# Attention and mixture of experts on one core: expert ranks by turns, two product groups in a bank, the overflow list by partitions

## The chip, the cores and the metric

The program runs on one core of a Trainium2 chip. The metric is the device time of a run in microseconds (us). Engines: PE is TensorE, with PEld its weight loads; DVE is VectorE, ACT ScalarE, POOL GpSimd, SP SyncE, whose queue issues most of the transfers.

## What is computed

Clustered attention on 4 batches, 8 heads, 768 positions of 64: queries and keys get the nearest of 16 centroids, and a query sees the keys of its own. The 3072 tokens of 512 numbers then go through 4 groups of 4 experts, one expert a token:

```python
for g in range(G):
    xg = x[g_idx == g]
    ...
    for e in range(Eg):
        ...
        h = np.maximum(xg[mask_e] @ w1[g, e], 0.0)
        ye = h @ w2[g, e]
        ...
        out[tok_idx] = combined[:, None] * ye
```

`w1[g, e]` is 512 x 1024, `w2[g, e]` 1024 x 512.

## The kernel before

Attention takes the first 400 us and isn't touched, apart from constants that POOL makes in it (`setup`, L985, near 98 us). Matrices are kept as two float16 parts, high and low, and a product of two is three matmuls.

The largest expert is begun early ("part A", 288 tokens, and a rest of 128 that is called rank -1). The other 15 are sorted by their count of tokens (`order`, L1327). Rank k has a fixed capacity `caps[k]` (L976): 288 for the largest, 272, 256 and so on down to 160 and 160. Tokens over the capacity go to an overflow list (`lists`, L1366, `make_list`, L1413), which `rest` works off at the end if it isn't empty; here it is.

`ranks` (L1464) runs rank -1 to 14. In a step, `up` (L1223) of rank k and `down` (L1242) of rank k-1 take turns, 12 matmuls each. `up` makes 8 groups of 12 matmuls, M = `caps[k]` columns each, into PSUM banks `psh` (three, a group a bank). ACT evicts a group as `hh`, DVE the rest as `hl` (L1238, L1239). `down` makes four groups of 24 into `psy` (two banks), evicted by ACT as `yh` and by DVE as `yl` (L1261, L1262); `settle` (L1284) turns them back to rows with products on `back`, ACT scales them to `y` (L1300) and POOL scatters the rows (L1301). For capacities of 240, 256 and 128 `feature_major` (L1278) picks the other form, 512-column products and no settle.

Around this, in fixed places of a step: POOL gathers the tokens of the next rank (L1193); PE transposes them and ACT copies them to `xT` (L1208, L1209); `stream` (L1159) loads the weights in chunks of 512 KB, six ahead, and splits them: the high part on ACT or POOL (L1019, L1021), the low part on DVE (L1022). The weights of two ranks fit at a time. `late` hands out one piece of the list a step, from rank 2 on (L1491 to L1493), on DVE, with one partition. The bank pool `psm` has three banks, for transposes, settles and the small products.

The order of instructions on each engine is set by a scheduler, from the order of the program and what it reckons each takes. An engine works off its instructions in that order.

Of the kernel before, what the change touches and what calls it, by code (L numbers as in the profile page):

```python
# [11 lines left out]
F16 = mybir.dt.float16  # L12
# [10 lines left out]
P = 128  # L23
# [929 lines left out]
class Experts:  # L953
# [13 lines left out]
    def __init__(self, ctx, tc, R, w1, w2, out, stage, wa):  # L967
        self.tc, self.R, self.w1, self.w2, self.out = tc, R, w1, w2, out
        self.nc = tc.nc
        self.D = out.shape[1]  # L970
        self.F = math.prod(w1.shape[1:]) // self.D
        self.stage, self.wa, self.stage2, self.nst = stage, wa, None, 0
        E = R.E
        const = self.const = ctx.enter_context(tc.tile_pool(name="econst", bufs=1))
        nc = self.nc
        self.caps = [288, 272, 256, 240, 232, 224, 216, 208, 200, 192, 184, 176, 168, 160, 160, self.CA]  # L976
        assert max(self.caps) == SL and len(self.caps) == E and not any(c % 8 for c in self.caps)
        self.sizes = [[min(P, c - t * P) for t in range(-(-c // P))] for c in self.caps]
        sm = self.small = lambda name, shape, dt=F32: const.tile(shape, dt, name=name)
        self.oh0 = sm("oh0", [P, E])  # L980
        self.cntA = sm("cntA", [P, E])
        self.f0f = sm("f0f", [P, 1])
        self.f0i = sm("f0i", [P, 1], I32)

    def setup(self):  # L985
        nc, const, E = self.nc, self.const, self.R.E
        self.io = const.tile([P, E], F32, name="io")
        nc.gpsimd.iota(self.io, [[1, E]], base=0, channel_multiplier=0, allow_small_or_imprecise_dtypes=True)
        self.capr = const.tile([1, E], F32, name="capr")
# [233 lines left out]
    def up(self, xT, M, W, h):  # L1223
# [5 lines left out]
        h += [hh, hl]  # L1229
        for f in range(FC):  # L1230
            fs = slice(f * P, (f + 1) * P)
            ph = next(self.ps_h).tile([P, 512], F32, name="psh")
            i = 0
            for k in range(KD):
                for w, a in ((w1h, 0), (w1h, 1), (w1l, 0)):
                    self.mm = nc.tensor.matmul(out=ph[:, 0:M], lhsT=w[:, k, fs], rhs=xT[:, a, k], start=i == 0, stop=i == 3 * KD - 1)  # L1236
                    i += 1
            nc.scalar.activation(out=hh[:, f], in_=ph[:, 0:M], func=AF.Relu)  # L1238
            self.ev = nc.vector.scalar_tensor_tensor(out=hl[:, f], in0=ph[:, 0:M], scalar=0.0, in1=hh[:, f], op0=ALU.max, op1=ALU.subtract)  # L1239
            yield  # L1240

    def down(self, h, M, W, gcols, idcols):  # L1242
# [4 lines left out]
        if self.feature_major(M):  # L1247
# [79 lines left out]
    def order(self):  # L1327
# [9 lines left out]
        c = sm("ocol", [V, 2])  # L1337
        nc.vector.tensor_tensor(out=t, in0=key, in1=R.emask, op=ALU.mult)
# [4 lines left out]
        nc.vector.scalar_tensor_tensor(out=self.pick, in0=self.io[0:V].unsqueeze(1).broadcast_to([V, 2, E]), scalar=c[:, 1:2], in1=R.wv.broadcast_to([V, 2, E]), op0=ALU.is_equal, op1=ALU.mult)  # L1343
# [22 lines left out]
    def lists(self):  # L1366
# [15 lines left out]
        yield
        done = self.done = sm("done", [1, E + 1])
        nc.vector.tensor_tensor(out=pe, in0=t.broadcast_to([1, E, E]), in1=self.io[0:1].unsqueeze(1).broadcast_to([1, E, E]), op=ALU.is_equal)
        nc.vector.tensor_tensor(out=pe, in0=pe, in1=self.capr.unsqueeze(1).broadcast_to([1, E, E]), op=ALU.mult)
        nc.vector.tensor_reduce(out=done[:, 0:E], in_=pe, axis=AX.X, op=ALU.add)
        nc.vector.memset(done[:, E:E + 1], float(self.CB))
        self.eid = sm("eid", [1, E + 1])
        nc.vector.tensor_copy(out=self.eid[:, 0:E], in_=self.io[0:1])
        nc.vector.tensor_copy(out=self.eid[:, E:E + 1], in_=self.f0f[0:1])  # L1390
        EB, MJ = E + 1, R.N // P + 1
        MO = self.MO = R.N // P + EB
        self.base = sm("base", [1, EB])
        self.jt = sm("jt", [1, EB, MJ])
        self.jj = sm("jj", [1, MO, EB], F16)
        with self.tc.issue_after(self.got.ins):
            self.iotas(EB, MJ, MO)
        for nm, sh in (("rem", [1, EB]), ("nov", [1, EB]), ("hiE", [1, EB]), ("loE", [1, EB]), ("zer", [1, EB]),
                       ("tmp", [1, MO, EB]), ("lst", [1, 2, MO]), ("sb", [1, EB])):
            setattr(self, "L" + nm, sm("L" + nm, sh))  # L1400
        self.Lgj = self.Ltmp.rearrange("o m e -> o (m e)")[:, 0:EB * MJ].rearrange("o (e m) -> o e m", m=MJ)
        self.Lind = sm("Lind", [1, MO, EB], F16)
        self.Llsi = sm("Llsi", [1, 2, MO], I32)
        self.Lnoi = sm("Lnoi", [1, 1], I32)
        nc.vector.memset(self.Lzer, 0.0)
        yield
        yield from self.make_list()

    def iotas(self, EB, MJ, MO):
        for t, pat in ((self.jt, [[0, EB], [P, MJ]]), (self.base, [[self.R.BS, EB]]), (self.jj, [[1, MO], [0, EB]])):  # L1410
            self.nc.gpsimd.iota(t, pat, base=0, channel_multiplier=0, allow_small_or_imprecise_dtypes=True)

    def make_list(self):  # L1413
        nc, R = self.nc, self.R
        EB, MJ, MO = R.E + 1, R.N // P + 1, self.MO
        V = nc.vector
        V.tensor_tensor(out=self.Lrem, in0=self.c17[0:1], in1=self.done, op=ALU.subtract)
        V.tensor_tensor(out=self.Lgj, in0=self.Lrem.broadcast_to([1, EB, MJ]), in1=self.jt, op=ALU.is_gt)
        V.tensor_reduce(out=self.Lnov, in_=self.Lgj, axis=AX.X, op=ALU.add)
        V.tensor_tensor_scan(out=self.LhiE, data0=self.Lnov, data1=self.Lzer, initial=0.0, op0=ALU.add, op1=ALU.add)  # L1420
        V.tensor_tensor(out=self.LloE, in0=self.LhiE, in1=self.Lnov, op=ALU.subtract)
        yield
        b3 = lambda x: x.unsqueeze(1).broadcast_to([1, MO, EB])
        V.tensor_tensor(out=self.Lind, in0=self.jj, in1=b3(self.LloE), op=ALU.is_ge)
        V.tensor_tensor(out=self.Ltmp, in0=self.jj, in1=b3(self.LhiE), op=ALU.is_lt)
        V.tensor_tensor(out=self.Lind, in0=self.Lind, in1=self.Ltmp, op=ALU.mult)
        yield
        V.tensor_tensor(out=self.Ltmp, in0=self.Lind, in1=b3(self.eid), op=ALU.mult)
        V.tensor_reduce(out=self.Llst[:, 0], in_=self.Ltmp, axis=AX.X, op=ALU.add)
# [4 lines left out]
        V.scalar_tensor_tensor(out=self.Ltmp, in0=self.jj, scalar=float(P), in1=b3(self.Lsb), op0=ALU.mult, op1=ALU.add)  # L1434
        V.scalar_tensor_tensor(out=self.Ltmp, in0=self.Ltmp, scalar=1.0 / 8, in1=self.Lind, op0=ALU.mult, op1=ALU.mult)
        V.tensor_reduce(out=self.Llst[:, 1], in_=self.Ltmp, axis=AX.X, op=ALU.add)
        V.tensor_copy(out=self.Llsi, in_=self.Llst)
        V.tensor_copy(out=self.Lnoi, in_=self.LhiE[:, EB - 1:EB])
# [93 lines left out]
class Fixup:  # L1532
# [24 lines left out]
    def finish(self):  # L1557
# [4 lines left out]
        nc.vector.tensor_tensor(out=any_, in0=self.zf[0:1], in1=X.LhiE[:, X.R.E:X.R.E + 1], op=ALU.add)  # L1562
# [136 lines left out]
```

## Time and profile before

| | |
|---|---|
| median of 3 runs | 739.57 us (739.32 to 740.96) |
| the profiled execution | 742.52 us |
| its span | 740.7 us |
| PE, PEld busy | 97%, 84% |
| DVE, ACT, POOL busy | 80%, 66%, 67% |
| mean granted clock of PE | 0.997 |

The span runs from the first instruction to the last; the time of the execution has some 2 us around it. Busy times of PE are modelled, as its matmuls overlap: what a matmul costs is read from the distance of starts.

### The profile page before, as it was taken

Reading aid. Unit: us, or ns where it says so; the run is one execution under the profiler, and the core shown is the slowest. Engines: PE = TensorE matmul, PEld = TensorE weight load, DVE = VectorE, ACT = ScalarE, POOL = GpSimd, SP = SyncE. Lnnn points to the kernel's source line nnn. Section 1 sums busy time; section 2 is a strip of 40 time slices with the busy share of each in tenths; the row PEclk is TensorE's granted clock in tenths of the full one; section 3 lists DMA queues with packets and bytes.
Section 4 is the critical chain, followed back from the end, with each engine's and each line's share of the span. In section 5 each row is a group of like instructions: output and inputs, shape, how many; then the busy total and the mean of one; then the engine's idle time right before and its main releaser. Section 6 shows DMA issues by size and latency. Waiting matters only on the chain.

```text
span 740.7 us, 26722 instructions
## 1 busy us (share of the span) xinstructions
PE 720.3 (97%) x11106; PEld 619.1 (84%) x11106; DVE 596.1 (80%) x1216; ACT 486.0 (66%) x952; POOL 493.6 (67%) x491
## 2 busy tenths in 40 slices
PE   8899999999999999999999989999999999999996
PEld 4688788888888888888888677888789999999996
DVE  6899889899888997989876476767779889988961
ACT  7778877788778887677977275444454555555642
POOL 8899787777787877878786325354644688554542
PEclk9999999999999999999999999999999999999998
DMA  8955634435245351240521696866777678887921
GB/s 226 224 141 153 192 100 119 155 99 154 81 120 172 95 159 37 67 131 3 178 81 38 234 313 220 273 211 221 237 244 234 230 272 284 284 275 264 281 77 36
DMA packets 45881, 128.04 MB, mean 173 GB/s; under 512 B 7699, under 2 KB 12691, under 8 KB 45752
## 3 DMA queue, kind: packets, MB, share of 16 engines
q1 hardware_dynamic: 40668, 112.64, 49.8%
q0 software_dynamic: 4928, 13.59, 5.1%
q8 instruction: 89, 1.46, 0.8%
q14 instruction: 40, 0.33, 0.1%
q10 hardware_dynamic: 156, 0.03, 0.0%
HBM read 93.41 MB, written 13.65 MB: 145 GB/s over the span
## 4 chain that ended last, share of the span: by engine, by line
PE 67%; DVE 17%; ACT 6%; issue 5%; DMA 2%; POOL 1%; another core or an unknown queue 1%; POOLq 0%; ACTq 0%; DVEq 0%
PE psh L1236 16%; PE psy L1258 12%; DVE mpart L382 7%; PE pso L447 6%; PE psf L421 6%; PE pso L448 5%; PE psf L422 5%; PE psc L379 5%; PE psy L1272 3%; DVE parts L224 2%; ACT p L426 2%; DMA st<-w 2%; PE psm L765 2%; PE psm L1294 1%; PE psm L1208 1%
## 5 line engine op out<-in xcount | busy, mean ns | idle before, releaser
L428 POOL TENSOR_TENSOR pl<-p 128x512 f16<-128x512 f32 x278 | 285.4, 1042 | 75.1 <-ACT p L426 70.6
L382 DVE TENSOR_REDUCE mpart<-psc 128x1 f32<-128x512 f32 (+1 forms) x282 | 190.2, 682 | 28.8 <-PE psc L379 28.4
L426 ACT ACTIVATE p<-psf 128x512 f32<-128x512 f32 x288 | 169.7, 596 | 45.6 <-PE psf L422 40.4
L447 PE MATMUL pso<-V,p 128*128 128x65 f16 x1152 | 160.2, 193 | 0.0
L448 PE MATMUL pso<-V,pl 128*128 128x64 f16 x1152 | 159.9, 193 | 0.0
L447 PE MATMUL pso<-V,pl 128*128 128x65 f16 x1152 | 159.4, 193 | 0.5 <-POOL pl L428 0.5
L448 PE MATMUL pso<-V,p 128*128 128x64 f16 x1152 | 159.3, 193 | 0.0
L421 PE MATMUL psf<-A 82*128 82x384 f16 (+2 forms) x576 | 142.5, 273 | 1.7 <-ACT p L426 1.6
L422 PE MATMUL psf<-B 128*128 128x384 f16 (+2 forms) x576 | 142.7, 273 | 0.0
L448 PEld LDWEIGHTS <-p 128*128 128x128 bf16 x1152 | 112.2, 97 | 22.2
L447 PEld LDWEIGHTS <-p 128*128 128x128 bf16 x1152 | 113.1, 98 | 9.6 <-issue 1.6
L447 PEld LDWEIGHTS <-pl 128*128 128x128 f16 x1152 | 112.5, 98 | 0.6 <-POOL pl L428 0.6
L448 PEld LDWEIGHTS <-pl 128*128 128x128 f16 x1152 | 111.5, 97 | 0.3
L379 PE MATMUL psc<-A 80*128 80x512 f16 (+1 forms) x376 | 106.3, 325 | 1.9 <-DVE mpart L382 1.2
L1239 DVE SCALAR_TENSOR_TENSOR hl<-psh,hh 128x160 f16<-128x160 f32 (+14 forms) x136 | 49.8, 368 | 48.9 <-ACT hh L1238 43.5
L1238 ACT ACTIVATE hh<-psh 128x160 f16<-128x160 f32 (+14 forms) x136 | 45.8, 345 | 59.1 <-PE psh L1236 54.9
L1301 POOL DMA_INDIRECT out_dram<-y,ri x33 | 43.4, 1316 | 52.4 <-ACT y L1300 46.3
L1236 PE MATMUL psh<-xT,wh0a 128*128 128x288 f16 (+7 forms) x512 | 74.6, 255 | 0.0
L1193 POOL DMA_INDIRECT xg<-xbuf,ri x25 | 40.5, 1620 | 43.7 <-PE psm L1208 30.1
L422 PEld LDWEIGHTS <-B 128*128 128x128 f16 x576 | 56.5, 98 | 10.9 <-issue 2.3
L1236 PE MATMUL psh<-xT,wh0b 128*128 128x272 f16 (+6 forms) x448 | 64.7, 253 | 0.0
L1236 PE MATMUL psh<-xT,wl0a 128*128 128x288 f16 (+7 forms) x256 | 64.0, 255 | 0.0
(385 smaller groups left out, 1785.9 us busy)
## 6 DMA issues: line engine op xcount, KB each, us to landing
st<-w SPq DMA_DIRECT2D x128, 512.0 KB
B<-parts SPq DMA_DIRECT2D x60, 192.0 KB
kx<-kT SPq DMA_DIRECT2D x16, 384.0 KB
qx<-qT SPq DMA_DIRECT2D x16, 384.0 KB
vx<-vr SPq DMA_DIRECT2D x16, 384.0 KB
xbuf<-xs SPq DMA_DIRECT2D x4, 1536.0 KB
A<-parts SPq DMA_DIRECT2D x30, 192.0 KB
A<-mk SPq DMA_DIRECT2D x56, 24.0 KB
```

What stands on the lines that cost most here:

```text
L379: last["mm"] = nc.tensor.matmul(out=pc[:, off:off + k1 - k0], lhsT=QA[h % 8][0:80, c * P:(c + 1) * P], rhs=KA[h % 8][0:80, k0:k1], start=T ...
L382: nc.vector.tensor_reduce(out=(mp[:, 0, 0:1], mp[:, :, 1], mp[:, 1, 0:1])[i], in_=pc.rearrange("p (a x) -> p a x", a=n), axis=AX.X, op=ALU ...
L421: nc.tensor.matmul(out=o, lhsT=KA[h % 8][0:82, ks], rhs=QA[h % 8][0:82, q0:q1], start=True, stop=False)
L422: nc.tensor.matmul(out=o, lhsT=KBs[h][:, ks], rhs=QBs[h][:, q0:q1], start=False, stop=True)
L426: cfg["exp"] = nc.scalar.activation(out=p32, in_=pf, func=AF.Exp, scale=QK / (SQ * SQ))
L428: lo = (nc.vector if u in (EARLY if h < 2 else DVE_LO[h % 8] if h < NH - 2 else DVE_END) else nc.gpsimd).tensor_tensor(out=pl, in0=p32, in ...
L447: nc.tensor.matmul(out=O[:, col:col + 65], lhsT=p[:, bs], rhs=vh, start=c == 0 and q == 0 and i == 0, stop=False, skip_group_check=True)
L448: nc.tensor.matmul(out=O[:, col:col + 64], lhsT=p[:, bs], rhs=vl, start=False, stop=c == NCH - 1 and i == 1, skip_group_check=True)
L1236: self.mm = nc.tensor.matmul(out=ph[:, 0:M], lhsT=w[:, k, fs], rhs=xT[:, a, k], start=i == 0, stop=i == 3 * KD - 1)
L1238: nc.scalar.activation(out=hh[:, f], in_=ph[:, 0:M], func=AF.Relu)
L1239: self.ev = nc.vector.scalar_tensor_tensor(out=hl[:, f], in0=ph[:, 0:M], scalar=0.0, in1=hh[:, f], op0=ALU.max, op1=ALU.subtract)
L1258: self.mm = nc.tensor.matmul(out=py[:, 0:M], lhsT=w[:, f, d * P:(d + 1) * P], rhs=a[:, f], start=i == 0, stop=i == len(prods) - 1)
```

## The change

Three edits. (1) `turn` takes the sorted ranks by turns: the largest, the smallest but one, the second, and so on; the capacities from rank 0 are now 288, 160, 272, 168, 256, 176, 240, 184, 232, 192, 224, 200, 216, 208, 160. `at` holds the same table for the chip, which `order` compares with. (2) Where 2M is at most 512, `up` and the feature-major `down` put two groups side by side into one bank, and evict both with one instruction on ACT and one on DVE. (3) The list is made with 128 partitions, an entry on each: operations of 17 columns take the place of ones of up to 697 on one partition, and sums over partitions are small products on PE: `dp`, `np_` and two for `lp`. The three iotas of `lists` go; `setup` makes `at`, `base` and `rows`.

```diff
-        self.caps = [288, 272, 256, 240, 232, 224, 216, 208, 200, 192, 184, 176, 168, 160, 160, self.CA]
+        caps = [288, 272, 256, 240, 232, 224, 216, 208, 200, 192, 184, 176, 168, 160, 160]
+        self.turn = [k // 2 if k % 2 == 0 else E - 3 - k // 2 for k in range(E - 2)] + [E - 2, E - 1]
+        self.caps = [caps[r] for r in self.turn[:-1]] + [self.CA]
...
+        two = 2 if 2 * M <= 512 else 1
         for f in range(FC):
             fs = slice(f * P, (f + 1) * P)
-            ph = next(self.ps_h).tile([P, 512], F32, name="psh")
+            if f % two == 0:
+                pair = next(self.ps_h).tile([P, 512], F32, name="psh")[:, 0:two * M].rearrange("p (t m) -> p t m", m=M)
...
-            nc.scalar.activation(out=hh[:, f], in_=ph[:, 0:M], func=AF.Relu)
-            self.ev = nc.vector.scalar_tensor_tensor(out=hl[:, f], in0=ph[:, 0:M], scalar=0.0, in1=hh[:, f], op0=ALU.max, op1=ALU.subtract)
+            if f % two == two - 1:
+                fs = slice(f + 1 - two, f + 1)
+                nc.scalar.activation(out=hh[:, fs], in_=pair, func=AF.Relu)
+                self.ev = nc.vector.scalar_tensor_tensor(out=hl[:, fs], in0=pair, scalar=0.0, in1=hh[:, fs], op0=ALU.max, op1=ALU.subtract)
...
+                if d % two == two - 1:
+                    ds = slice(d + 1 - two, d + 1)
+                    self.yev.append(nc.scalar.activation(out=yh[:, ds], in_=pair, func=AF.Copy, scale=1.0 / YS))
+                    nc.vector.scalar_tensor_tensor(out=yl[:, ds], in0=pair, scalar=1.0 / YS, in1=yh[:, ds], op0=ALU.mult, op1=ALU.subtract)
...
+        dp = R.psm.tile([P, 512], F32, name="psm")
+        nc.tensor.matmul(out=dp[:, 0:E], lhsT=dw, rhs=R.ident[0:E, 0:E], start=True, stop=True)
...
+        V.tensor_tensor(out=self.Lrem, in0=self.c17, in1=self.done, op=ALU.subtract)
+        V.tensor_scalar(out=self.Lgt, in0=self.Lrem, scalar1=step, scalar2=None, op0=ALU.is_gt)
+        np_ = R.psm.tile([P, 512], F32, name="psm")
+        nc.tensor.matmul(out=np_[:, 0:EB], lhsT=R.ones, rhs=self.Lgt, start=True, stop=True)
+        yield
+        V.tensor_copy(out=self.Lnov, in_=np_[:, 0:EB])
...
+        lp = R.psm.tile([P, 512], F32, name="psm")
+        for w in range(2):
+            nc.tensor.matmul(out=lp[0:1, w * MO:(w + 1) * MO], lhsT=self.Llst[:, w:w + 1], rhs=R.identf[:, 0:MO], start=True, stop=True)
```

Three places show how it moves instructions. First DVE where the list finds what is over (`Lrem`), before:

```order
L1239 SCALAR_TENSOR_TENSOR hl<-psh,hh 128x232
L1022 SCALAR_TENSOR_TENSOR wl1b<-st,wh1b 128x4x256
L1417 TENSOR_TENSOR Lrem<-c_12838,done 1x17
L1418 TENSOR_TENSOR Ltmp<-Lrem,jt 1x425
L1419 TENSOR_REDUCE Lnov<-Ltmp 1x17
L1239 SCALAR_TENSOR_TENSOR hl<-psh,hh 128x232
```

and now, in the rank of 256 (a pair has 512 columns; the lines are those of the changed kernel):

```order
L1255 SCALAR_TENSOR_TENSOR hl<-psh,hh 128x512
L1034 SCALAR_TENSOR_TENSOR wl1b<-st,wh1b 128x4x256
L1432 TENSOR_TENSOR Lrem<-c_12820,done 128x17
L1282 SCALAR_TENSOR_TENSOR yl<-psy,yh 128x336
L1433 TENSOR_SCALAR Lgt<-Lrem,rows 128x17
L1034 SCALAR_TENSOR_TENSOR wl0a<-st,wh0a 128x2x512
```

The reduction that gave `Lnov` on DVE is gone; `Lgt` goes to PE instead. There, where before nothing stood between the products of `up`, it is now, with what each waits for:

```order
L1276 MATMUL psy<-hh,wl1a 128x168
L1250 LDWEIGHTS wh0a
L1250 MATMUL psh<-xT,wh0a 128x256
L1435 LDWEIGHTS ones [waits DVE_49]
L1435 MATMUL psm<-Lgt,ones 128x17 [waits Activation_49]
L1250 LDWEIGHTS wh0a
```

This is one product into the sixth group of `up`; 12 products of `down` (168 columns, L1276), the fifth group and 12 of `down` again stand behind the fourth group, whose pair the `hl` above evicts. Last, ACT at the end of the last rank, before:

```order
L1300 ACTIVATE y<-psm,rg 128x512
L1300 ACTIVATE y<-psm,rg 32x512
L1261 ACTIVATE yh<-psy 128x160 x4
L1300 ACTIVATE y<-psm,rg 128x512
L1300 ACTIVATE y<-psm,rg 32x512
```

and now:

```order
L1320 ACTIVATE y<-psm,rg 128x512
L1320 ACTIVATE y<-psm,rg 80x512
L1281 ACTIVATE yh<-psy 128x320 x2
L1320 ACTIVATE y<-psm,rg 128x512
L1320 ACTIVATE y<-psm,rg 32x512
```

Four evictions of a group have become two of a pair; a product on `back` that reads one half of a pair now stands on PE behind the eviction of both.

## Rows read from the trace of the kernel before

**Rows 1.** The page, busy time, share of the span, instructions

```profile
span 740.7 us, 26722 instructions
...
PE 720.3 (97%) x11106; PEld 619.1 (84%) x11106; DVE 596.1 (80%) x1216; ACT 486.0 (66%) x952; POOL 493.6 (67%) x491
```

**Rows 2.** Windows from one rank's first `up` product to the next's

```profile
core 0: us, PE busy (x) PEld busy (x) DVE busy (x) ACT busy (x) POOL busy (x), PEclk, DMA share, GB/s
...
460.76:484.54 23.78, 23.78 (x211) 19.68 (x208) 16.95 (x22) 10.87 (x20) 11.06 (x12) 1.00 0.81 267
...
609.59:627.96 18.37, 18.37 (x226) 18.37 (x225) 17.70 (x30) 10.20 (x20) 15.10 (x10) 1.00 0.84 274
627.96:645.69 17.73, 17.73 (x227) 17.73 (x226) 16.35 (x27) 9.84 (x20) 10.37 (x8) 1.00 0.89 293
...
695.25:711.20 15.95, 15.84 (x235) 15.70 (x233) 13.49 (x25) 8.58 (x21) 7.91 (x6) 1.00 0.69 217
```

**Rows 3.** Chain of waits in order of time (start, us, what)

```profile
445.66 1.47 PE psh L1236 x12
...
654.51 0.95 PE psh L1236 x12
```

**Rows 4.** Timeline around three pauses (start, length, engine, line, idle before)

```profile
434.79 0.38 PE L1272 MATMUL psy<-wl1a,hh 128*128 128x512 f16 x1
...
435.30 0.68 DVE L1239 SCALAR_TENSOR_TENSOR hl<-psh,hh 128x128 f16<-128x128 f32 x3
...
435.63 0.27 PE L1236 MATMUL psh<-xT,wh 128*128 128x128 f16 x2 [0.46 <-DVE hl L1239]
...
683.50 0.35 DVE L1262 SCALAR_TENSOR_TENSOR yl<-psy,yh 128x184 f16<-128x184 f32 x1 [1.60 <-ACT yh L1261]
683.53 0.24 PE L1236 MATMUL psh<-xT,wl0a 128*128 128x168 f16 x1
683.90 0.77 PE L1258 MATMUL psy<-hh,wh1a 128*128 128x176 f16 x8
...
699.37 0.34 DVE L1262 SCALAR_TENSOR_TENSOR yl<-psy,yh 128x176 f16<-128x176 f32 x1 [0.53 <-ACT yh L1261]
...
699.41 0.23 PE L1236 MATMUL psh<-xT,wl0b 128*128 128x160 f16 x1
699.76 0.45 PE L1258 MATMUL psy<-hh,wh1b 128*128 128x168 f16 x4
```

**Rows 5.** Groups by shape, 440 us on (xcount, busy us, mean ns, idle)

```profile
L1022 DVE SCALAR_TENSOR_TENSOR wl1b<-st,wh1b 128x1024 f16<-128x1024 f32 x30 | 44.7, 1489 | 0.0
L1239 DVE SCALAR_TENSOR_TENSOR hl<-psh,hh 128x160 f16<-128x160 f32 x16 | 5.1, 318 | 7.2 <-ACT hh L1238 7.1
L1239 DVE SCALAR_TENSOR_TENSOR hl<-psh,hh 128x288 f16<-128x288 f32 x8 | 3.6, 454 | 5.0 <-ACT hh L1238 3.0 <-ACT wh1b L1019 1.9
...
L1238 ACT ACTIVATE hh<-psh 128x160 f16<-128x160 f32 x16 | 4.8, 306 | 8.3 <-PE psh L1236 6.9 <-issue 1.4
L1238 ACT ACTIVATE hh<-psh 128x288 f16<-128x288 f32 x8 | 3.2, 403 | 3.4 <-PE psh L1236 3.4
```

**Rows 6.** Timeline at the end of the last rank

```profile
733.08 0.33 DVE L1262 SCALAR_TENSOR_TENSOR yl<-psy,yh 128x160 f16<-128x160 f32 x1 [1.51 <-ACT yh L1261]
...
733.47 0.29 PE L1294 MATMUL psm<-back,yl 128*128 128x128 f16 x2
```

**Rows 7.** Groups of DVE, the list's lines, 460 to 700 us

```profile
L1424 DVE TENSOR_TENSOR Lind<-jj,LloE 1x697 f16<-1x697 f16 x1 | 0.9, 872 | 0.0
...
L1417 DVE TENSOR_TENSOR Lrem<-c,done 1x17 f32<-1x17 f32 x1 | 0.2, 159 | 0.0
```

**Rows 8.** Timeline of POOL near 98 us

```profile
98.60 0.15 POOL L988 IOTA io<- 128x16 f32 x1
```

**Rows 9.** Lines L1553 and L1554 (ns min/median/max, first and last start)

```profile
L1553 PE MATMUL psm<-zh,ones x1: 167/167/167, 636.9 to 636.9; 128*128 128x1 f16 x1
...
L1554 DVE COPY zf<-psm x1: 145/145/145, 640.3 to 640.3; 128x1 f32<-128x1 f32 x1
```

More of the change, by code (lines that the diff above doesn't have):

```diff
@@ L975, in __init__ @@
         nc = self.nc
-        self.caps = [288, 272, 256, 240, 232, 224, 216, 208, 200, 192, 184, 176, 168, 160, 160, self.CA]
-        assert max(self.caps) == SL and len(self.caps) == E and not any(c % 8 for c in self.caps)
+        caps = [288, 272, 256, 240, 232, 224, 216, 208, 200, 192, 184, 176, 168, 160, 160]
+        self.turn = [k // 2 if k % 2 == 0 else E - 3 - k // 2 for k in range(E - 2)] + [E - 2, E - 1]
+        self.caps = [caps[r] for r in self.turn[:-1]] + [self.CA]
+        assert sorted(self.turn) == list(range(E)) and max(self.caps) == SL and len(self.caps) == E and not any(c % 8 for c in self.caps)
         self.sizes = [[min(P, c - t * P) for t in range(-(-c // P))] for c in self.caps]
@@ L1386, in lists @@
[L1386 to L1402, printed above, removed]
+        V = nc.vector
@@ new lines, in lists @@
+        EB, MO = E + 1, R.N // P + E + 1
+        self.MO = MO
+        c = self.c17 = sm("c17", [P, EB])
+        t = sm("lt", [P, E])
+        V.tensor_tensor(out=t, in0=R.cnt, in1=self.oh0, op=ALU.mult)
+        V.tensor_reduce(out=c[:, E:EB], in_=t, axis=AX.X, op=ALU.add)
+        V.tensor_tensor(out=t, in0=self.cntA, in1=R.cnt, op=ALU.subtract)
+        V.tensor_tensor(out=t, in0=t, in1=self.oh0, op=ALU.mult)
+        V.tensor_tensor(out=c[:, 0:E], in0=R.cnt, in1=t, op=ALU.add)
+        dn = sm("dn", [E, E])
@@ L1403, in lists @@
+        V.tensor_copy(out=done[:, 0:E], in_=dp[:, 0:E])
+        V.memset(done[:, E:EB], float(self.CB))
+        self.eid = sm("eid", [P, EB])
+        V.tensor_copy(out=self.eid[:, 0:E], in_=self.io)
+        V.tensor_copy(out=self.eid[:, E:EB], in_=self.f0f)
+        for nm in ("rem", "nov", "hiE", "loE", "zer", "tmp", "sb", "ind"):
+            setattr(self, "L" + nm, sm("L" + nm, [P, EB]))
+        self.Lgt = sm("Lgt", [P, EB], F16)
+        self.Llst = sm("Llst", [P, 2])
         self.Llsi = sm("Llsi", [1, 2, MO], I32)
@@ L1404, in lists @@
         self.Lnoi = sm("Lnoi", [1, 1], I32)
[L1405 removed]
+        V.memset(self.Lzer, 0.0)
         yield
         yield from self.make_list()
[L1409 to L1411 removed]
     def make_list(self):
         nc, R = self.nc, self.R
[L1415 removed]
+        EB, MO = R.E + 1, self.MO
@@ L1416, in make_list @@
         V = nc.vector
-        V.tensor_tensor(out=self.Lrem, in0=self.c17[0:1], in1=self.done, op=ALU.subtract)
-        V.tensor_tensor(out=self.Lgj, in0=self.Lrem.broadcast_to([1, EB, MJ]), in1=self.jt, op=ALU.is_gt)
-        V.tensor_reduce(out=self.Lnov, in_=self.Lgj, axis=AX.X, op=ALU.add)
+        row, step = self.rows[:, 0:1], self.rows[:, 1:2]
+        V.tensor_tensor(out=self.Lrem, in0=self.c17, in1=self.done, op=ALU.subtract)
+        V.tensor_scalar(out=self.Lgt, in0=self.Lrem, scalar1=step, scalar2=None, op0=ALU.is_gt)
@@ L1424, in make_list @@
[L1424 to L1429, printed above, removed]
+        V.tensor_scalar(out=self.Ltmp, in0=self.LloE, scalar1=row, scalar2=None, op0=ALU.is_le)
@@ L1430, in make_list @@
+        V.scalar_tensor_tensor(out=self.Lind, in0=self.LhiE, scalar=row, in1=self.Ltmp, op0=ALU.is_gt, op1=ALU.mult)
+        V.tensor_tensor(out=self.Ltmp, in0=self.Lind, in1=self.eid, op=ALU.mult)
+        V.tensor_reduce(out=self.Llst[:, 0:1], in_=self.Ltmp, axis=AX.X, op=ALU.add)
         yield
```

65 lines of the change are left out of this document (33 added, 32 removed).

## The prediction, made before the changed kernel ran

> **What bounds the kernel now.** I read four views in this order: the page's busy times, the windows (one stretch per rank of the expert part), the chain of waits, and the timeline wherever TensorE (PE) pauses. The span is 740.7 us and PE is busy 97% of it [rows 1]. A busy PE need not be at its pace, so the windows come next, cut where each rank's `up` begins: from 460.76 to 711.20 us PE's busy time equals the stretch to 0.2 us, at a granted clock of 1.00, which is the 2.4 GHz level [rows 2]. The chain confirms it by start times: a group of 12 products of 288 columns takes 1.47 us, 122 ns each, and one of 184 columns 0.95 us, 79 ns each [rows 3]; that is columns / 2.4 GHz plus 2 to 2.5 ns. So a rank costs what its columns cost. VectorE (DVE) is nearly full in some stretches, 17.70 of 18.37 us [rows 2], but PE never slows with it, except at the few pauses below. The expert part is PE's, and only what changes PE's work, its pauses or the end after its last product can show.
>
> **The turns: 0 us.** The caps are the same numbers in another order, the choice of `down`'s form depends on the cap alone, and gathers, transposes and settles go with the cap. A stretch holds `up` of one rank and `down` of the one before. Before, stretches shrink from 23.78 to 15.95 us [rows 2]; by the pitch above, 96 products of 160 columns (6.6 us), 96 of 288 (11.8 us) and some 1.3 us of transposes and settles make about 19.7 us, so now all are near 19. Sum: unchanged. The demand on the weight stream (eight 512 KB chunks a rank) becomes even; the shortest stretch before already held at 15.95 us with PE full, so 19 us should be covered by the transfers and splits. If that cover failed, it would be in the early ranks (rival C).
>
> **The pairs: -1.1 us of pauses.** Two groups now share a bank, so two `psy` banks hold four groups and three `psh` banks six. Three pauses show what that frees: PE stops after 683.53 until 683.90 while DVE's `yl` of 683.50 to 683.85 frees the bank; the same at 699.41 to 699.76; and at 434.79 to 435.63 it waits for `hl`, three small evictions behind a split [rows 4]. Less one pitch each (0.07, 0.07 and 0.22 us) that is 0.30, 0.28 and 0.62 us. I take the first two whole, and 0.5 of the last, since ScalarE (ACT) is full there too: -1.1, at most -1.2, at least -0.6.
> An eviction of 160 columns takes 318 ns on DVE and 306 on ACT, of 288 columns 454 and 403 [rows 5]: 1.06 and 0.76 ns a column, with some 0.15 and 0.18 us for each instruction. Some 78 instructions fewer on either engine (56 of `up`, 22 of `down`) are about 12 us of DVE and 14 of ACT. They are worth 0 beyond the pauses, because PE runs at its pace without them.
> [...]
> At the end pairing costs: the last two groups of the last rank are evicted only together. Before, `yl` of 160 columns began at 733.08, and the settling product that reads it started at 733.47 [rows 6]. Now ACT takes 306 + 160 x 0.76 = 428 ns and DVE 318 + 160 x 1.06 = 488 ns, so 0.29 us more before the last settling products, of which two more than before then remain ahead of the first output copy (0.11 us): **+0.4 us**, between 0.3 and 0.6.
>
> **The list.** Its long one-partition operations, such as 872 ns for 697 elements, give way to ones of 17 columns; one of these took 159 ns [rows 7]. DVE gains over 10 us, worth 0 as above. The iotas that leave GpSimd (POOL) late cover nothing. Seven small instructions and one memset more on POOL near 98 us, at 0.15 us for an iota [rows 8], make at most 1.2 us there, beside an attention pass in which POOL's long operations wait for ACT; I take 0.
> New on PE are four small products (`dp`, `np_`, two of `lp`). The nearest row is the 167 ns of the one-column product on `ones` [rows 9], whose busy time includes its drain; so 0.2 to 0.7 us for four, and I take **+0.4**.
> Three of the four read what DVE made a rank or several evictions earlier. `np_` does not: it reads `Lgt`, which stands on DVE behind `hl` of a 512-column pair, a weight split, `Lrem` and `yl`, in the rank of 256 columns, and the product stands one product into the sixth group of `up` (order shown above). Both sides from the last product of the fourth group: PE has 12 products of 168 columns twice (0.87 us each; in between 12 of 256, 1.31 us) and one more, 3.2 us. DVE has ACT's eviction (about 0.2 us to start, 0.57 long), `hl` 0.69, the split 1.49 [rows 5], `Lrem` 0.16, `yl` of 336 columns 0.50 and `Lgt` 0.16: 3.8 us if nothing queues, and ACT's own split ahead of it may add some. So PE stands still, with every product of the rank behind it: 0.6 us, up to 3 where DVE is as far behind as it was at 640.3 us, when it copied a product started at 636.9 [rows 9]; nothing if the split was done early. I take **+1.0 us**, the nearer end plus part of a queue.
> `np_`'s bank is held for a whole rank; two of three stay for settles and transposes, which here come two at a time: 0.
>
> **Sum.** 0 - 1.1 + 0.4 + 0.4 + 1.0 = +0.7 us. The profiled execution took 742.52 us, so 743.2; the runs' median stands 2.95 us under it, at 739.57: **740.3 us**. All terms at their good ends make -0.7 (738.9); 1.8 us at `np_` and the others at their bad ends +2.5 (742.1). A measurement of this kernel tells a change of over 0.2%, 1.48 us, from none.
>
> **Rivals.**
> A, slower: the wait at `np_` is long. It decides once DVE is about 1 us further behind there than reckoned. For it: DVE lagged 3.4 us at 636.9 to 640.3 [rows 9]. Against it: that was in a fuller stretch, and pairs and turns make this one lighter. At a stall of 3.3 us instead of 1.0: 742.6 us. Chance 0.20.
> B, faster: pauses beyond the three go as well, because a DVE with 12 us less to do releases PE earlier. Against it: PE is full from 460 to 711 us, so only the transition before 443 us has room; with no stall at `np_` and 0.8 us more won there, 740.3 - 1.8 = 738.5, and below 738.1 it counts as faster. Chance 0.10 for faster.
> C, slower: the stream cannot follow, as the second stretch shrinks from 23.78 us to 19.7. Eight chunks are 4.2 MB, 213 GB/s over 19.7 us, against 293 GB/s seen at 627.96 us [rows 2]; if that stretch kept its old length, +4.1, 744.4 us. Chance 0.05.
> That the order does not change as described is excluded by the order of instructions shown above.
>
> **How the numbers follow.** My case, within 0.2%, has 0.65; B 0.10; A 0.20 and C 0.05. The range takes in my case and most of A and B, and leaves out C and their far ends: 738.4 to 742.7.
>
> **What would show it.** The chain should hold the same sum of PE time, with stretches near 19 us; no pause of PE behind `yl` or `hl`; one pause of about 1 us at the product on `Lgt`, near 530 us; DVE's busy time down by some 20 us with no effect; the last `yl` as one of 320 columns, 0.4 us later. It is wrong if PE loses time in many places (pairs evicted too late for the next rank), if the early stretches wait for chunks, or if the time falls by more than the pauses hold.

## The result, and the profile after

The changed kernel took 744.35 us (median of 5 runs, 743.12 to 746.97) against 739.57 us: the ratio is 1.0064, 95% interval 1.0041 to 1.0087, so 3 to 6.4 us slower. Two later measurements gave 1.0068 (1.0046 to 1.0091) and 1.0059 (1.0039 to 1.0079). In all later measurements, on four chips, the kernel before took 742.2 to 742.7 us; so below a ratio is always to the kernel before as it was timed beside the run.

The profiled executions hide most of it. That of before stood 2.95 us over the median of its runs, that of the change 1.2 us under, and the spans differ by 0.7 us only. The page of the changed kernel, beside [rows 1]:

```profile
span 741.4 us, 26582 instructions
...
PE 720.0 (97%) x11112; PEld 619.1 (84%) x11112; DVE 573.5 (77%) x1136; ACT 476.9 (64%) x874; POOL 477.6 (64%) x496
```

PE's busy time is the same to 0.3 us, DVE has 23 us less to do. So the loss is PE standing still, and the pauses are the distance of two starts less the pitch (0.417 ns a column and 2.5 ns, worked out from the two groups of [rows 3]; 2.4 columns a ns, which the prediction writes as 2.4 GHz). The pauses in us, before, in this profile, and in a third profile of the changed kernel (the run `after_c` below):

| place (us of the span) | before | change | `after_c` |
|---|---|---|---|
| part A waits for `yl`, near 424 | 1.86 | 0 | 2.06 |
| rank -1: bank wait, then `xT`, 434 to 440 | 0.63 + 0.46 | 0 + 1.61 | 0 + 1.11 |
| nothing the profile shows, 441 to 446 | 1.28 | 0 | 0.37 |
| `hl` or `hh` late, 455 and 463 | 0 | 0 | 0.32 + 0.92 |
| the product on `Lgt` | - | 1.95 | 1.94 |
| first `down` products wait for `hh`, near 560 and 598 | 0 | 0.79 + 0.21 | 0.96 + 0 |
| `psy` bank, 683 to 731 | 0.76 | 0 | 0 |
| settle of the last rank but one waits for the paired `yl` | 0 | 0.29 | 0.29 |
| last `down` product to the end of the span | 8.2 | 8.8 | 9.1 |

Only the first profile of the change lacks the first row: every other profile of either kernel and of all variants has 1.6 to 2.1 us there. With it, this execution would lie 0.6 us over the median of its runs instead of 1.2 us under.

The windows by rank, beside [rows 2] (columns as there):

```profile
core 0: us, PE busy (x) PEld busy (x) DVE busy (x) ACT busy (x) POOL busy (x), PEclk, DMA share, GB/s
...
457.38:476.87 19.49, 19.49 (x218) 17.12 (x216) 14.61 (x17) 9.63 (x17) 10.57 (x9) 1.00 0.91 304
...
516.70:538.12 21.42, 19.63 (x236) 18.31 (x234) 14.00 (x18) 9.87 (x15) 10.90 (x9) 1.00 0.76 258
...
557.50:576.06 18.56, 17.93 (x210) 17.34 (x208) 13.23 (x18) 9.88 (x15) 9.12 (x8) 1.00 0.76 254
...
651.96:671.05 19.09, 19.09 (x226) 19.09 (x225) 14.28 (x17) 9.66 (x16) 9.15 (x7) 1.00 0.79 271
```

The stretches are even, as the turns mean, and PE is full in most. The rank of 256 (516.70) holds 1.8 us without PE. The waits name it, from 440 to 735 us:

```profile
PEld L1435 <- DVE Lgt L1433: 2.0, 1, 2.0
PE psm L1435 <- DVE Lgt L1433: 1.8, 1, 1.8
...
PE psy L1276 <- ACT hh L1254: 0.6, 1, 0.6
```

What made `Lgt` late stands in the timeline, DVE's and POOL's instructions and the product:

```profile
527.17 0.69 DVE L1255 SCALAR_TENSOR_TENSOR hl<-psh,hh 128x512 f16<-128x512 f32 x1 [1.94 <-ACT hh L1254]
...
527.78 1.22 DVE L1034 SCALAR_TENSOR_TENSOR wl1b<-st,wh1b 128x1024 f16<-128x1024 f32 x1
...
528.52 1.38 POOL L1033 TENSOR_SCALAR wh0a<-st 128x1024 f16<-128x1024 f32 x1
...
528.91 1.01 DVE L1432 TENSOR_TENSOR Lrem<-c,done 128x17 f32<-128x17 f32 x1
...
529.84 0.49 DVE L1282 SCALAR_TENSOR_TENSOR yl<-psy,yh 128x336 f16<-128x336 f32 x1
529.87 1.04 POOL L1033 TENSOR_SCALAR wh1a<-st 128x1024 f16<-128x1024 f32 x1
530.26 0.69 DVE L1433 TENSOR_SCALAR Lgt<-Lrem,rows 128x17 f16<-128x17 f32 x1
...
531.00 0.18 PE L1435 MATMUL psm<-Lgt,ones 128*128 128x17 f16 x1 [1.79 <-DVE Lgt L1433]
```

The queue is the one that the prediction gave, but `Lrem` takes 1.01 us and `Lgt` 0.69 where [rows 7] have 0.16 for such an operation, on one partition and with nothing on POOL beside it. Each ends when a split on POOL ends: 529.92 beside 529.90, 530.95 beside 530.91.

The other new wait is ACT's, ahead of the first `down` of the rank of 176 columns:

```profile
557.57 1.06 ACT L1031 ACTIVATE wh1b<-st 128x1024 f16<-128x1024 f32 x1 [2.36 <-DMA st<-w]
558.53 1.04 ACT L1031 ACTIVATE wh0b<-st 128x1024 f16<-128x1024 f32 x1
559.48 0.44 ACT L1254 ACTIVATE hh<-psh 128x352 f16<-128x352 f32 x1
...
559.97 0.31 PE L1276 MATMUL psy<-hh,wh1a 128*128 128x176 f16 x2 [0.63 <-ACT hh L1254]
```

The last `hh` of the rank stands on ACT behind two splits, and the first of these waits for its chunk. The kernel before has the same order on ACT,

```profile
529.36 1.06 ACT L1019 ACTIVATE wh1b<-st 128x1024 f16<-128x1024 f32 x1 [1.36 <-DMA st<-w]
530.32 1.04 ACT L1019 ACTIVATE wh0b<-st 128x1024 f16<-128x1024 f32 x1
531.27 0.35 ACT L1238 ACTIVATE hh<-psh 128x240 f16<-128x240 f32 x1
```

in the step where `up` of 240 columns runs beside the 512-column `down` of the rank of 256. That step is 22.4 us long (508.32 to 530.68), and PE waits for nothing. Now 176 columns run beside this `down`, in 19.4 us (538.12 to 557.50).

The end, beside [rows 6]:

```profile
732.91 0.44 ACT L1281 ACTIVATE yh<-psy 128x320 f16<-128x320 f32 x1 [2.88 <-PE psy L1276]
733.38 0.49 DVE L1282 SCALAR_TENSOR_TENSOR yl<-psy,yh 128x320 f16<-128x320 f32 x1 [2.83 <-ACT yh L1281]
...
733.93 0.23 PE L1314 MATMUL psm<-back,yl 128*128 128x128 f16 x1 [0.24 <-DVE yl L1282]
```

### The profile page after: what moved, and what is told of

It reads as the page before. It is cut to its first block, busy times and chain, and to the rows that moved or that the text cites. A ratio compares the mean times of both kernels' runs of the same rounds, so it can differ in the third digit from the quotient of the medians.

```text
span 741.4 us, 26582 instructions
## 1 busy us (share of the span) xinstructions
PE 720.0 (97%) x11112; PEld 619.1 (84%) x11112; DVE 573.5 (77%) x1136; ACT 476.9 (64%) x874; POOL 477.6 (64%) x496
## 4 chain that ended last, share of the span: by engine, by line
PE 66%; DVE 17%; ACT 5%; issue 5%; DMA 4%; POOL 1%; SPq 0%; ACTq 0%; POOLq 0%; DVEq 0%
PE psh L1250 17%; PE psy L1276 13%; DVE mpart L382 6%; PE pso L447 5%; PE pso L448 5%; PE psf L421 5%; PE psf L422 5%; PE psc L379 5%; PE psy L1292 3%; DVE parts L224 2%; ACT p L426 2%; PE psm L1314 2%; PE psm L765 1%; PE psm L1220 1%; DMA st<-w 1%
## 5 line engine op out<-in xcount | busy, mean ns | idle before, releaser
L1255 DVE SCALAR_TENSOR_TENSOR hl<-psh,hh 128x288 f16<-128x288 f32 (+14 forms) x80 | 42.1, 527 | 71.1 <-ACT hh L1254 71.0
L1250 PE MATMUL psh<-xT,wh0a 128*128 128x288 f16 (+7 forms) x512 | 81.5, 264 | 0.0
L1321 POOL DMA_INDIRECT out_dram<-y,ri x33 | 40.6, 1229 | 62.1 <-ACT y L1320 57.0
L1254 ACT ACTIVATE hh<-psh 128x288 f16<-128x288 f32 (+14 forms) x80 | 37.0, 463 | 59.7 <-PE psh L1250 59.6
L1250 PE MATMUL psh<-xT,wl0a 128*128 128x288 f16 (+7 forms) x256 | 67.0, 264 | 0.0
L421 PEld LDWEIGHTS <-A 82*128 82x128 f16 x576 | 55.7, 98 | 9.2 <-issue 1.1
L1250 PE MATMUL psh<-xT,wh0b 128*128 128x160 f16 (+6 forms) x448 | 57.9, 243 | 0.0
```

The costliest lines, as they stand in the source:

```text
L421: nc.tensor.matmul(out=o, lhsT=KA[h % 8][0:82, ks], rhs=QA[h % 8][0:82, q0:q1], start=True, stop=False)
L1250: self.mm = nc.tensor.matmul(out=pair[:, f % two], lhsT=w[:, k, fs], rhs=xT[:, a, k], start=i == 0, stop=i == 3 * KD - 1)
L1255: self.ev = nc.vector.scalar_tensor_tensor(out=hl[:, fs], in0=pair, scalar=0.0, in1=hh[:, fs], op0=ALU.max, op1=ALU.subtract)
L1321: d = nc.gpsimd.indirect_dma_start(out=self.out, out_offset=bass.IndirectOffsetOnAxis(ap=idc, axis=0), in_=y[0:n], in_offset=None, bounds_ ...
```

## The experiments

Each was timed beside the kernel before (median us of both; ratio, 95% interval).

### Each part alone

`turns` has the new order of capacities and nothing else, `pairs` only the shared banks, `list` only the list by partitions. In the terms of the change's diff, `turns` keeps the old `up`, `down` and list; `list` is the change with

```diff
-        self.turn = [k // 2 if k % 2 == 0 else E - 3 - k // 2 for k in range(E - 2)] + [E - 2, E - 1]
+        self.turn = list(range(E))
...
-        two = 2 if 2 * M <= 512 else 1
+        two = 1
```

> Only the turns, without pairs and with the list as it was. Theory of pauses (what the change costs is PE standing still at single places: 1.95 us at the product on Lgt, 0.8 and 0.2 us before two down passes that wait for hh, 0.4 us at the end): no term of it is in this kernel, so within 0.7 us of before. Theory of the stream (turns make the ranks from the second on ask for their weight chunks sooner, so splits and then hh come late): 2 to 4 us slower than before, with pauses of PE behind hh or a split between 460 and 600 us.

> Only the pairs. Theory of pauses: the bank waits go (-0.6 us), the last eviction is 0.4 us later, hh of a pair can be late for the next down by a few tenths: between 0.5 us faster and 1 us slower than before. Theory of granularity (a pair's eviction starts a group later, so every handover from up to down loses): 2 us or more slower.

> Only the list by partitions, ranks in the old order, no pairs. Theory of pauses: one pause at the product on Lgt of 1 to 2.5 us and 0.4 us for the small products: 1.4 to 2.9 us slower than before, PE released there by DVE. Theory of the stream: within 0.5 us of before.

| run | this / before | ratio |
|---|---|---|
| `turns` | 745.30 / 742.26 | 1.0037 (1.0022 to 1.0051) |
| `pairs` | 742.57 / 742.26 | 1.0004 (0.9989 to 1.0019) |
| `list` | 742.88 / 742.26 | 1.0003 (0.9988 to 1.0019) |

The turns alone cost 2.7 us (1.6 to 3.8), as the theory of the stream had it. The theory of pauses was wrong on them, because I had counted the pauses at 560 and 598 us as the pairs'. Their profile has them, 1.84 and 0.41 us, at the same place:

```profile
559.44 1.06 ACT L1026 ACTIVATE wh1b<-st 128x1024 f16<-128x1024 f32 x1 [3.41 <-DMA st<-w]
560.41 1.04 ACT L1026 ACTIVATE wh0b<-st 128x1024 f16<-128x1024 f32 x1
561.35 0.30 ACT L1245 ACTIVATE hh<-psh 128x176 f16<-128x176 f32 x1
...
561.70 0.24 PE L1265 MATMUL psy<-hh,wh1a 128*128 128x176 f16 x1 [1.68 <-ACT hh L1245]
```

The pairs do free the bank, and win nothing (0.3 us slower, -0.8 to 1.4). In their profile the wait of 0.63 us for `hl` is gone, but the settling product behind ACT's copy to `xT` waits 1.10 us instead of 0.46. PE begins rank 0 at 441.70, 1.8 us earlier than before if both are counted from part A's first product (403.3 and 402.9 us); at the next rank's start (461.26; before, 460.76 [rows 2]) 0.1 us late. The gain went into pauses of rank 0, among them this one (0.40 us on PE, by `hl`):

```profile
453.86 1.06 ACT L1019 ACTIVATE wh1a<-st 128x1024 f16<-128x1024 f32 x1 [4.22 <-DMA st<-w]
454.82 0.39 ACT L1242 ACTIVATE hh<-psh 128x288 f16<-128x288 f32 x1
...
455.25 0.46 DVE L1243 SCALAR_TENSOR_TENSOR hl<-psh,hh 128x288 f16<-128x288 f32 x1 [3.73 <-ACT hh L1242]
```

It is the same pattern: an eviction on ACT behind a split that waits for its chunk. 1.14 us more are pauses at 445 to 447 us with no cause in the profile; before, such pauses (1.28 us) stand at 442 us, ahead of rank 0, so most of the earlier start is only a pause that moved behind it.

The list alone shows a pause of 1.80 us at the product on `Lgt`, yet it was 0.2 us slower than before (-0.9 to 1.4) and not the 1.4 to 2.9 expected; why that pause shows in the profile and not in the time stays open. No split of POOL runs beside `Lrem` and `Lgt` there, and they take 0.17 and 0.24 us; of DVE's two splits ahead of them one took 1.90 us and the other 1.27. `list_np` is `list` with the product a rank later:

> The list by partitions alone, with the product on Lgt a rank later. Theory of pauses: the 1.8 us pause that the run with the list alone shows near 542 us goes and nothing else moves, so within 0.6 us of before, though DVE has 12 us less to do. If a lighter DVE is worth something by itself: 1 us or more faster than before.

742.69 / 742.65, ratio 1.0000 (0.9985 to 1.0015), the pause gone. DVE is busy for 589.9 us there, so the list relieves it of 6 us and not of 12; that relief is worth nothing, as reckoned.

### The product on `Lgt`

```diff
         V.tensor_scalar(out=self.Lgt, in0=self.Lrem, scalar1=step, scalar2=None, op0=ALU.is_gt)
+        yield
         np_ = R.psm.tile([P, 512], F32, name="psm")
```

> The change with the product on Lgt one rank later (a yield between Lgt and the product). Theory of pauses: the 1.95 us at that product go, 2 us faster than the change, some 742.4 us. Theory of the stream (PE is paced by the chunks over longer stretches, a local pause is made up for later): as the change, 744 us.

743.99 / 742.26, ratio 1.0014 (0.9999 to 1.0029), where the change itself has 1.0059 to 1.0068: the pause is gone from the profile, and the intervals do not meet. (That 743.99 us is also the 744 of the other theory means nothing: the change did not run beside it, and by its ratios it would have taken 746.6 to 747.3 us there.) The gain is then 2.6 to 3.3 us, more than the pause. The change again:

> The changed kernel once more, beside the others of this call. Its first profile lacked a pause of 1.7 to 1.9 us near 424 us that the kernel before and all four variants show, where PE waits for an eviction of part A and no engine is busy. If that pause comes and goes by itself, it is there this time or in most executions, and the span is 742 to 744 us; the pauses near 529 us (about 2 us) and 559 us (0.5 to 1 us) must return in the same places, as they follow from the order of instructions. Against before: 3 to 5 us slower.

746.31 / 742.16, ratio 1.0068 (1.0046 to 1.0091). The pause near 424 us was there (1.84), that at the product was 1.95 us again, that near 560 us 0.33 us only, with 1.8 us of pauses between 444 and 462 us.

To see why the product waits 1.95 us and not the 0.6 of the plain queue, `pool_q1` moves to ACT the two splits that POOL works on meanwhile. The order on PE is the same, row for row, and so is that on DVE until one `hl` near 643 us.

```diff
-                self.split_chunk(st, *self.weights_of(r, i), i, q, self.HI[(n - self.AHEAD + 1) % 8] if n - self.AHEAD + 1 >= self.LEAD else 0)
+                self.split_chunk(st, *self.weights_of(r, i), i, q, 0 if (r, i) in ((6, 0), (5, 1)) and q == 1 else self.HI[(n - self.AHEAD + 1) % 8] if n - self.AHEAD + 1 >= self.LEAD else 0)
```

> The change, with two chunk splits of one rank moved from POOL to ACT, those that run on POOL while DVE makes Lrem and Lgt. Theory of the shared path (these two operations of DVE wait while POOL works on its split): Lrem takes 0.17 us instead of 1.01, Lgt 0.24 instead of 0.69, and the pause at the product falls from 1.95 to about 0.7 us; the time is 1.3 us under that of the change, if nothing comes late on ACT for its two splits more. Theory that the queue on DVE alone is the cause: Lrem and Lgt stay as long and so does the pause.

> The change once more, on the same chip as the run beside it: 4 to 5 us slower than before, Lrem 1.01 and Lgt 0.69 us long, the pause 1.95 us.

`pool_q1` 744.90 / 742.15, ratio 1.0032 (1.0017 to 1.0048); `after_c` 747.24 / 742.15, 1.0059 (1.0039 to 1.0079). In `pool_q1` the pause is 0.67 us, and DVE reads

```profile
529.87 1.23 DVE L1034 SCALAR_TENSOR_TENSOR wl1b<-st,wh1b 128x1024 f16<-128x1024 f32 x1
531.03 0.17 DVE L1432 TENSOR_TENSOR Lrem<-c,done 128x17 f32<-128x17 f32 x1
531.12 0.49 DVE L1282 SCALAR_TENSOR_TENSOR yl<-psy,yh 128x336 f16<-128x336 f32 x1
531.53 0.23 DVE L1433 TENSOR_SCALAR Lgt<-Lrem,rows 128x17 f16<-128x17 f32 x1
```

So 1.3 of the 1.95 us come from POOL's two splits; that is shown. The medians differ by 2.3 us. The intervals of the ratios overlap, but 9 of the 12 runs of `pool_q1` are faster than the fastest of `after_c`, timed beside it.

### The turns and the token-major step

`turns_late` is `turns` with the first four ranks left in place, so that the ranks of 256 and 240 keep long steps; `turns_fm` is `turns` with the feature-major `down` for them:

```diff
-        self.turn = [k // 2 if k % 2 == 0 else E - 3 - k // 2 for k in range(E - 2)] + [E - 2, E - 1]
+        self.turn = [0, 1, 2, 3] + [4 + k // 2 if k % 2 == 0 else E - 3 - k // 2 for k in range(E - 6)] + [E - 2, E - 1]
```

```diff
-        return 3 * KD * FC * M + 2 * nt * D < 3 * nt * FC * D
+        return M > P
```

> Only turns, but from the fifth rank on: 288, 272, 256, 240 keep their places, then largest and smallest by turns. Theory of the token-major step (in the step that runs the 512-column form of down beside up, ACT has two splits ahead of the last hh, and the first of them waits for a chunk; with 176 or 184 columns beside it the step is 3 us shorter than with 240 or 232 and PE reaches the hh first): the two steps are as long as before, both pauses near 560 and 599 us go, within 0.7 us of before. Theory of even demand (the stream is short of bandwidth wherever steps of 19 us take the place of longer ones): pauses behind hh or splits turn up in the new even stretch from 550 us on, 1.5 us or more slower than before.

> All turns, but ranks of 256 and 240 columns use the feature-major form of down as the others do (some 1.4 us more work on PE: 2560 columns, 64 products of settle and more instructions). Theory of the token-major step: no pause of PE behind hh near 560 and 599 us (2.25 us in the run with turns alone), so 0.5 to 1.5 us faster than that run, some 744.5 us where it had 745.3. Theory of even demand: the pauses stay or move, and the time is 1 us above that run or more.

`turns_late` 742.67 / 742.16, ratio 1.0009 (0.9998 to 1.0020); `turns_fm` 742.57 / 742.16, 1.0006 (0.9995 to 1.0016), although its PE has, by the estimate above, some 1.4 us more work. Both pauses are gone in either. In `turns_late` ACT's three instructions stand in the same order, and PE loses nothing there; in `turns_fm` one split and not two is ahead of the last `hh` (a bank wait of 0.44 us near 555 us, for `yl`, is new there). The theory of even demand falls: the even stretches of `turns_late` cost nothing that can be told from before (0.7 us, -0.1 to 1.5).

If the chunk's lateness counts and not ACT's order alone, one more chunk buffer must do as well. The change gets a seventh:

```diff
-    AHEAD = 6
+    AHEAD = 7
...
-        pool = self.stage2 if self.stage2 and self.nst % 3 == 0 else self.stage
+        pool = self.stage2 if self.stage2 and self.nst % 7 in (0, 2, 4) else self.stage
...
-        self.stage2 = ctx.enter_context(tc.tile_pool(name="stage2", bufs=2))
+        self.stage2 = ctx.enter_context(tc.tile_pool(name="stage2", bufs=3))
```

> The change with a seventh buffer for weight chunks, so that a chunk is asked for one split earlier; ACT's order at the two token-major steps is that of the change. Theory of the late chunk (PE waits for an hh that stands on ACT behind a split whose chunk has not landed): the pauses of the change behind hh and hl near 454, 461, 560 and 598 us shrink to under a third; the 2 us at the product on Lgt and the end stay, so some 1.5 us faster than the change and 2 to 4 us slower than before. Theory that ACT's order alone costs it, however early the chunk: pauses near 560 and 598 us stay as they are.

743.87 / 742.65, ratio 1.0021 (1.0004 to 1.0039). The pauses near 454, 560 and 598 us are gone, 0.27 us is left near 461; ACT's order at the step is unchanged, and its first split waits 0.17 us in place of 2.36:

```profile
558.06 1.06 ACT L1031 ACTIVATE wh1b<-st 128x1024 f16<-128x1024 f32 x1 [0.17 <-DMA st<-w]
559.03 1.04 ACT L1031 ACTIVATE wh0b<-st 128x1024 f16<-128x1024 f32 x1
559.97 0.44 ACT L1254 ACTIVATE hh<-psh 128x352 f16<-128x352 f32 x1
```

So the chunk's lateness counts: with ACT's order unchanged the pause is gone. The time is 1.6 us over before (0.3 to 2.9), a little less than the 2 to 4 expected; its interval ends where the change's begin, at 1.0039 to 1.0046.

### The repairs together

`np_tail` is the change with the product a rank later and the last rank's `down` unpaired (`two = 2 if 2 * M <= 512 and not last else 1`); `np_tail_a7` has seven buffers too; `best1` is `np_tail` with the order of `turns_late`, `best1_a7` with seven buffers as well, `noturn_a7` is `np_tail_a7` in the old order. `np_tail_a8` and `best1_a8` have eight buffers.

> The change with three repairs: the product on Lgt a rank later, turns only from the fifth rank on, and the last rank's down not paired. Theory of pauses: of the change's losses (about 2, 1 and 0.4 us) none is left, so within 1 us of before, 3 us or more faster than the change. If pairs or the list cost in some way that no single pause shows, it stays 1.5 us or more slower than before.

> The change with the product on Lgt a rank later and the last down not paired, six chunk buffers, all turns. Theory of pauses: 2 and 0.8 us of the change's 5 are gone, the pauses behind hh near 454, 461, 560 and 598 us (1 to 2 us) stay: 1 to 2.5 us slower than before. If there is a cost that shows in no single pause: 3 us or more slower.

> The same with seven chunk buffers. Theory of pauses with the late chunk: those four pauses go too and the 1.5 us that pairs win before the first rank are kept: between as before and 1.5 us faster. Against it: eight buffers cost 5 us by a stall at the start of the stream; if seven do the same in part, PE stands still near 437 us and it is slower than before.

> Turns from the fifth rank on only, otherwise as the last. If turns cost nothing once the chunk is early, this and the last agree within 0.7 us; if all turns still cost, this one is 1 us faster or more.

> Pairs and the list with the same repairs and seven chunk buffers, ranks in the old order. If the turns give nothing by themselves (PE's columns are the same in any order), it agrees with the two above within 0.7 us; if even steps are worth something, it is 1 us slower than they are or more.

> The change with all turns kept, the product on Lgt a rank later, the last down not paired and eight chunk buffers. Theory of the late chunk: nothing of the change's losses is left but tenths, and what the pairs win before 443 us is kept: between 1.5 us faster than before and 0.5 us slower. If turns are costly however early chunks are asked for: 1.5 us slower than before or more.

> The version with three repairs (product later, turns from the fifth rank on, last down not paired) and eight chunk buffers. It was 0.6 us slower than before with six. Theory of the late chunk: its two pauses near 443 and 453 us (0.6 us together) go and the 1.5 us that pairs win before the first rank are kept: 0.5 to 1.5 us faster than before. If pairs' gain is eaten by something other than chunks: as before within 0.5 us.

| run | this / before | ratio |
|---|---|---|
| `best1` | 742.56 / 742.16 | 1.0008 (0.9997 to 1.0019) |
| `np_tail` | 742.80 / 742.37 | 1.0005 (0.9989 to 1.0022) |
| `np_tail_a7` | 741.78 / 742.37 | 0.9993 (0.9980 to 1.0006) |
| `best1_a7` | 741.52 / 742.37 | 0.9985 (0.9972 to 0.9998) |
| `noturn_a7` | 741.74 / 742.37 | 0.9984 (0.9970 to 0.9999) |
| `np_tail_a8` | 747.52 / 742.65 | 1.0063 (1.0040 to 1.0086) |
| `best1_a8` | 746.19 / 742.65 | 1.0043 (1.0026 to 1.0060) |

Without the early product and the last pair nearly the whole loss is gone: `np_tail` is back at the time of before, with all turns in it. It was expected 1 to 2.5 us slower, and is 0.4 (-0.8 to 1.6). `best1`, timed beside `after_again`, took 742.56 us against its 746.31. In `np_tail` the two pauses near 560 and 598 us are still there (0.61 and 0.33 us), together under half of those of `turns`. DVE had worked there on three long operations of the old list, from 549.9 to 553.7 us; whether that is the reason was not tried. With seven buffers the two versions of fewer or no turns are 1.1 and 1.2 us faster than before, at the edge of their intervals, and agree with `np_tail_a7` within 0.7 us: the turns give nothing. These are the best versions that were run.

Eight buffers went against both expectations: measured against before, the kernels are 2.6 and 4.3 us slower than with six. Both profiles have a new stall where the stream begins; in that of `best1_a8` ACT reads

```profile
435.88 1.06 ACT L1032 ACTIVATE wh0b<-st 128x1024 f16<-128x1024 f32 x1 [4.78 <-DMA st<-w]
436.85 0.39 ACT L1282 ACTIVATE yh<-psy 128x288 f16<-128x288 f32 x1
```

Part A's last `yh` stands behind a split that waits 4.78 us for its chunk. Why the chunk comes later with more buffers was not tried.

## Why the prediction was wrong

**What failed is the term at `np_` first.** "I take +1.0 us, the nearer end plus part of a queue": it measured 1.95 us in all three profiles of the change. The queue came out right in sum: without POOL's splits it leaves 0.67 us, beside the 0.6 reckoned. Part of that is luck: in `pool_q1` `hl` began 0.6 us later than reckoned, behind ACT's own split, and DVE's split took 1.23 us instead of 1.49, while each start overlapped the end before it by some 0.1 us. What was missing is that `Lrem` and `Lgt` ended only with POOL's splits beside them, 1.01 and 0.69 us long. I had priced them at 0.16 us by a row with one partition and no POOL beside it, and a long stall was put down to DVE's lag alone. Rival A named the place too, but again for DVE's lag, and even its price, 742.6 us, does not reach the 744.35 measured.

In the change both are recorded behind the start of a split on POOL, and took 1.01 and 0.69 us; in `pool_q1`, without these splits, 0.17 and 0.23. In `np_later` `Lgt` is recorded 0.34 us ahead of the first of two splits and still ends after the second. By what means a split holds them up no run shows. With the two measured lengths the term would have been 0.6 + 0.84 + 0.46 = 1.9 us.

The forecast fell 4.1 us short, and this term is 0.95 us of it. By the two later profiles the pairs' gain that did not stay is 0.9, the turns 0.3 to 1.0, and the end with the rank before it 0.5 to 0.8. Each of these follows below.

**The turns' 0 rested on the wrong cover.** "The shortest stretch before already held at 15.95 us with PE full, so 19 us should be covered" measures by a step without the 512-column `down`. (Its rank ends at 710.67 us, not at 711.20, so it held at 15.4 us; that does not help the argument.) The steps with the 512-column `down` need their chunk earlier against ACT's order, and were long before: the split ahead of the last `hh` waited 1.36 us for its chunk in a step of 22.4 us, without a pause of PE, and 2.36 in the change, in one of 19.4. Rival C (the stream cannot follow) named the resource, but its place and its price (one early stretch keeps its length) were others. Alone the turns cost 2.7 us; inside the change the profiles show 0.3 to 1.0 us there.

**The pairs' -1.1 did not stay won.** The bank waits went as said, at all three places. But a pause that goes is a gain only if PE's next partner is ahead. In ranks -1 and 0 the pauses were 2.4 us before and are 2.9 in the two later profiles of the change. ACT's copy to `xT` is part of it (1.11 instead of 0.46), and two evictions that stand on ACT behind a split with a late chunk (near 454 and 462 us, as in `pairs`) are 1.2 to 1.5; for the rest the profiles name no cause.

**The end, +0.4, was 0.6 to 0.9** (0.5 of it in the two new pauses there), and the rank before it lost 0.29 us in the same way: its settle also waits for a paired `yl`, which the prediction did not look at. **The small products, +0.4,** took 0.6 us with the short gaps around them, within their range of 0.2 to 0.7. **DVE's 20 us without effect was right:** 23 us in the whole change, and `list_np`, with 6 us less, is as fast as before.

**The sum and the median.** The spans differ by the +0.7 us of the prediction only by chance, through the pause near 424 us. I had seen that the profiled execution stood 2.95 us over the median, and carried its single pauses over as if every run had them.

What stays open: the product and the last pair cost 2.5 us by their own pauses, and 4.0 to 4.7 by the ratios of the change and of `np_tail`. Counted from part A's first product (402.9 us in the profile before) to the end of the span, before takes 337.8 us, `np_tail` 338.7, and the change 341.8 (`after_again`) and 342.8 (`after_c`). So the profiles hold the loss; beside those two terms it lies in pauses between 444 and 463 us, 1.8 us in either later profile of the change against 0.3 in `np_tail`. Most of these are the two evictions behind a late chunk. The first profile of the change has none of them, and no run shows why the chunk is late in some executions only.

## What to carry to other kernels

When one engine is full, ask of each pause that goes which partner sets the pace next, and look at every queue for an eviction that stands behind a transfer's wait: here such a pattern cost PE nothing in a step of 22.4 us, and 0.79 us in one of 19.4. A small operation whose result the full engine waits for is priced with what the neighbouring engines do at that moment, not by its own row from a quiet place: `Lrem` took 0.17 us with no split on POOL, and 1.01 beside one. A seventh buffer in the stream took away the pauses that the even order of work had brought; with eight the kernels were 2.6 and 4.3 us slower than with six.

## What the runs showed of the hardware

A DVE operation of 17 columns ended only with POOL's splits beside it: `Lgt` took 0.23 us with no split on POOL (`pool_q1`), 0.69 beside one (in the change, to 530.95 us, the split to 530.91), and in `np_later`, where two splits of POOL ran from 532.66 to 534.74 us, 2.46:

```profile
532.32 2.46 DVE L1433 TENSOR_SCALAR Lgt<-Lrem,rows 128x17 f16<-128x17 f32 x1
532.66 1.08 POOL L1033 TENSOR_SCALAR wh0a<-st 128x1024 f16<-128x1024 f32 x1
533.67 1.07 POOL L1033 TENSOR_SCALAR wh1a<-st 128x1024 f16<-128x1024 f32 x1
```

PE's granted clock fell where PE stood still with eight buffers. In `best1_a8` PE stood for 2.7 us from 437.1 us on and for 1.8 us from 441.0 on; the windows read (columns as in [rows 2])

```profile
430.00:440.00 10.00, 7.43 (x117) 6.93 (x116) 4.81 (x7) 5.22 (x8) 2.93 (x4) 0.97 0.86 329
440.00:445.00 5.00, 3.48 (x34) 3.32 (x33) 4.44 (x6) 4.85 (x9) 0.45 (x2) 0.50 0.84 295
445.00:450.00 5.00, 5.00 (x42) 3.85 (x41) 0.64 (x3) 3.48 (x6) 2.78 (x3) 0.87 0.73 281
450.00:455.00 5.00, 5.00 (x34) 3.09 (x33) 4.00 (x6) 2.03 (x4) 0.00 (x0) 1.00 0.40 125
```

At 0.50 three products of 128 columns took 0.32 us from start to start (440.10 to 440.42 us), ahead of the first pause 0.17 (435.51 to 435.68). By an estimate from the windows, the 0.97 of the first is some 0.6 us at 0.50, so the clock fell near 439.4 us, inside the first of the two pauses, and by the 0.87 it rose near 446.3. In `np_tail_a8` the clock read 1.00 from 436 to 440 us, where PE was busy for 1.42 us, 0.65 from there to 445 (busy for 2.87) and 0.66 from there to 450 (busy throughout). The single pause of 1.95 us at the product on `Lgt` left the clock at 1.00 (the window from 516.70 to 538.12 us).
